# Attention and gated MLP on one core: the first two batches in turns of two f tiles, a written-out opening, and two DMA queues with fixed contents

## The chip, the cores and the metric

The kernel runs on one core of one Trainium2 chip. The metric is the device time of one execution in microseconds (us). Three runs of the kernel before took 806.85, 806.34 and 803.88 us, median 806.34.

The engines are named as in the profile: PE (TensorE matmuls; PEld its weight loads), DVE (VectorE), ACT (ScalarE), POOL (GpSimd, which in this kernel mainly issues DMAs) and SP (SyncE, which only issues DMAs).

## What is computed

Eight batches, eight heads, 576 tokens, head size 64; a learned memory of 32 slots per head; then a gated MLP of width 1536 on the 512 features of every token.

```python
a = softmax(phi)                       # over the 32 slots
k_m = einsum('bhsm,bhsd->bhmd', a, k)  # 32 keys and values per head
v_m = einsum('bhsm,bhsd->bhmd', a, v)
attn = softmax(q @ k_m.T / 8)
x = (attn @ v_m)                       # to [4608 tokens, 512]
out = (sigmoid(x @ w_gate) * (x @ w_val)) @ w_out
```

The weights of the MLP arrive as 64-bit words and are turned into 32-bit floats on the chip.

## The kernel before

**Tiles.** The 1536 columns of the MLP are 12 *f tiles* of 128. A *step* is one f tile of one batch. `make_u` (line 395 ff.) multiplies v_m into the gate and value weights of one or two f tiles, which gives `u` (in a high and a low part, `u_hi`, `u_lo`). `gate_half` (line 419) multiplies the attention weights `at` (again `at_hi`, `at_lo`) by `u`: half c=0 takes 256 tokens, half c=1 takes 320. ACT forms the sigmoid, DVE the product `sg` (line 445), ACT and DVE split it in `g_hi` and `g_lo`. `out_half` (line 455) multiplies that by the output weights `wo` and adds it up in four PSUM tiles acc0 to acc3 of 128 tokens, two to a half. It follows its gate half by three halves (`LAG`).

**Turns.** A batch is worked on for a stretch of f tiles, a *turn*. Batches 0 to 3 take turns of four f tiles (steps 0 to 47: batches 0, 1, 2, 3 with f 0 to 3, then all four with f 4 to 7, then with f 8 to 11), batches 4 to 7 one turn of twelve (steps 48 to 95). At the end of a turn the four sums leave PSUM: DVE or ACT write them to a `row` tile (lines 471 to 476; two buffers), which is stored to DRAM as `part`. At the end of the next turn of the batch `row_of` (line 489) loads that part again, DVE adds it (line 471), and the row is stored as `part` or `out`. The rows of acc0 and acc1 are loaded ahead; those of acc2 and acc3 need the buffers that the stores of the first two free. The next turn needs acc0 to acc3 again about two halves later. `at` has two buffers, so a batch that comes back has its `at` loaded again (`again`).

**Attention** of a batch is: `a_max` and `a_exp` (softmax over phi; DVE and ACT), `memory` (PE transposes, k_m and v_m, more transposes), `scores` (PE, DVE transposes into `e`), `s_max`, `s_exp`, `normalize` and `turn` (DVE and ACT), which gives `at`. From batch 1 on these pieces are fed between the halves of the steps of another batch (`sides`, `go_on`).

**Weights.** A conversion (`to_f32`, line 162; ACT one operation, DVE four) is due at the step that the table `CONVERT` gives: jobs (f, 0) and (f, 1) make the gate and value weights of f tile f, job (f, 2) its `wo` (a cast on ACT and a subtraction on DVE more). The words of the next job are loaded as soon as one of three `words` buffers is free (one buffer for the last f tiles).

**Order.** The first part, up to line 626, is written out as `step(...)` calls, each of which is chained behind the one before on PE, DVE, ACT and POOL. After that PE's matmuls and ACT's activations with a table are chained in program order, and a scheduler places the other instructions. All loads but those of `part` are chained on SP's queue in program order (`load`, line 112): phi, k and v, q, the words, and `at` coming back. The loads of `part` (line 493) are on SP's queue too, placed freely. Stores (`store`, line 119) are on POOL's queue, placed freely.

Of the kernel before, what the change touches and what calls it, by code (L numbers as in the profile page):

```python
# [17 lines left out]
P = 128  # L18
# [19 lines left out]
ALONE = 4  # L38
# [14 lines left out]
def attn_moe_kernel(  # L53
# [56 lines left out]
    last_load = [None]  # L110

    def load(dst, src):

        with ExitStack() as behind:
            if last_load[0] is not None:
                behind.enter_context(tc.issue_after(last_load[0].ins))
            last_load[0] = nc.sync.dma_start(dst, src)  # L117

    def store(dst, src):

        nc.gpsimd.dma_start(dst, src)  # L121
# [26 lines left out]
    def load_jobs(n=None):  # L148

        while jobs and (n is None or n > 0):  # L150
            f, k = jobs[0]
            room = WORDS[len(wos) - 1]
            if (k == 2 and f // NE >= len(wos)) or len(waiting) == room:
                break
            src = wo[f] if k == 2 else wgv[f][:, 2 * k : 2 * k + 2, :].rearrange("p k n -> p (k n)")
            words = pools["conv"].tile([P, 512, 2], I32, name="words", bufs=room)
            load(words.rearrange("p n t -> p (n t)"), src.bitcast(I32))
            words_of[f, k] = words
            waiting.append(jobs.pop(0))
            n = n and n - 1  # L160
# [41 lines left out]
    def load_phi(b):  # L202
        ph = att([P, NG, S], "ph")
        load(ph, phiT[b])
        loaded[b, "phi"] = ph

    def load_kv(b):
        kt = att([P, 512], "kvt")
        load(kt, kvt[b])
        km = []  # L210
        for g in range(NG):
            t = att([P, SF, 512], f"kvm{g}")
            load(t, kvm[b, g])
            km.append(t)
        loaded[b, "kv"] = (km, kt)

    def load_q(b, cuts=(0, 1)):
        if 0 in cuts:
            loaded[b, "q"] = att([P, NKT * S], "q")
        for c in cuts:  # L220
            for u, n in PIECES[c]:
                o = u * NKT * 2 * P
                load(loaded[b, "q"][:, o : o + NKT * n], qT[b][:, o : o + NKT * n])
# [134 lines left out]
    def turn(b, c=None):  # L358
# [26 lines left out]
    def again(b):  # L385
        new_at(b)
        for d, a in zip(kept[b], at[b]):
            load(a.rearrange("p r n -> p (r n)").bitcast(F32), d)
# [66 lines left out]
    def out_half(b, f, c, at_start, at_end):  # L455
# [3 lines left out]
        for j in range(2):  # L459
# [8 lines left out]
            if at_end:  # L468
# [8 lines left out]
                if f == NFT - 1:  # L477
                    store(out[b * S + t * P : b * S + (t + 1) * P, :], st)
# [10 lines left out]
    def row_of(b, t):  # L489

        st = mb.tile([P, DM], F32, name="row", bufs=2)
        if (b, t) in part:
            nc.sync.dma_start(st, part[b, t])
        return st
# [6 lines left out]
    def out_left(pair, f0, nf):  # L501
# [66 lines left out]
    turns = [(b, f0, f0 + TURN) for f0 in range(0, NFT, TURN) for b in range(QUAD)]  # L568
# [17 lines left out]
    load_jobs(1)  # L586
    load_kv(0)
    load_jobs(1)
    load_q(0)
    load_phi(1)  # L590
    load_jobs(1)
    load_kv(1)
    load_jobs()
# [87 lines left out]
    for b in range(QUAD, B - 1):  # L681
# [5 lines left out]
        begin[turns[k - 1][:2]]: b for k, (b, f0, _) in enumerate(turns) if b < QUAD and f0  # L687
# [15 lines left out]
    pend = []  # L703
    for i, (b, f, at_start, at_end) in enumerate(steps):
        if i in sides:
            run(beside)
            beside, pieces = chain(*(g for _, g in sides[i])), sum(n for n, _ in sides[i])
            length = next(n for n in range(i + 1, len(steps) + 1) if n == len(steps) or steps[n][2]) - i
            slots = 2 * length - 1
# [3 lines left out]
        if i:  # L713
            gate_half(b, f, 0)
# [11 lines left out]
        if i:  # L726
            gate_half(b, f, 1)
# [64 lines left out]
```

## Time and profile before

| | |
|---|---|
| median of three runs | 806.34 us |
| the profiled execution's own time | 808.47 us |
| its span, first to last instruction | 806.7 us |
| mean granted TensorE clock | 0.965 |
| PE busy | 745.8 us (92%) |
| DVE busy | 435.2 us (54%) |
| ACT busy | 338.9 us (42%) |
| POOL busy | 44.4 us (6%) |
| bytes moved | 93.17 MB |

A row of a timeline gives the start in us, the duration, the engine, the line, the operation, output<-inputs with their shapes, and in brackets how long the engine had been idle and who released it. A row of the windows gives a stretch, then busy time (and count) of PE, PEld, DVE, ACT and POOL, then the granted clock, the share of the DMA engines and GB/s. A DMA's row is its issue; when it landed is told in the sixth part of the page.

### The profile page before, as it was taken

Reading aid. Unit: us, or ns where it says so; the run is one execution under the profiler, and the core shown is the slowest. Engines: PE = TensorE matmul, PEld = TensorE weight load, DVE = VectorE, ACT = ScalarE, POOL = GpSimd, SP = SyncE. Lnnn points to the kernel's source line nnn. Section 1 sums busy time; section 2 is a strip of 40 time slices with the busy share of each in tenths; the row PEclk is TensorE's granted clock in tenths of the full one; section 3 lists DMA queues with packets and bytes.
Section 4 is the critical chain, followed back from the end, with each engine's and each line's share of the span. In section 5 each row is a group of like instructions: output and inputs, shape, how many; then the busy total and the mean of one; then the engine's idle time right before and its main releaser. Section 6 shows DMA issues by size and latency. Waiting matters only on the chain.

```text
span 806.7 us, 13723 instructions
## 1 busy us (share of the span) xinstructions
PE 745.8 (92%) x5588; PEld 615.0 (76%) x5588; DVE 435.2 (54%) x840; ACT 338.9 (42%) x791; POOL 44.4 (6%) x86
## 2 busy tenths in 40 slices
PE   7447789998999999999999999999999999999995
PEld 5335568786788877888888888878888888888884
DVE  4788485958646655454754653356234643343422
ACT  3456354644734334333444443336333443333321
POOL 0000010110100100110010100000000000010001
PEclk9669889999999999999999999999999999999998
DMA  9754627363663544343245233002000100010001
GB/s 351 275 185 172 256 87 302 121 240 127 250 242 118 200 171 147 116 143 107 79 137 187 79 102 119 1 27 86 2 1 1 53 14 1 1 53 1 1 1 66
DMA packets 26879, 93.17 MB, mean 115 GB/s; under 512 B 3520, under 2 KB 4544, under 8 KB 24768
## 3 DMA queue, kind: packets, MB, share of 16 engines
q1 hardware_dynamic: 20160, 69.74, 24.5%
q0 software_dynamic: 6656, 22.55, 7.5%
q8 instruction: 44, 0.72, 0.4%
q14 instruction: 19, 0.16, 0.1%
HBM read 69.73 MB, written 22.54 MB: 114 GB/s over the span
## 4 chain that ended last, share of the span: by engine, by line
PE 56%; issue 20%; DMA 9%; DVE 8%; ACT 5%; POOL 1%; SPq 1%; POOLq 0%; DVEq 0%; ACTq 0%
PE pu_t L135 34%; PE acc L135 21%; DMA words<-in_wo_dram 6%; DMA words<-in_wgv_dram 3%; ACT L108 2%; DVE wg L172 1%; DMA kvm<-in_kvm_dram 1%; POOL out_dram L121 1%; DVE wg L175 1%; ACT ph L108 1%; SPq L117 1%; ACT wo_raw L167 0%; DVE sg L445 0%; ACT wg L167 0%; DVE wg L168 0%
## 5 line engine op out<-in xcount | busy, mean ns | idle before, releaser
L135 PE MATMUL pu_t<-at_hi,u_hi 128*128 128x256 f32 (+1 forms) x760 | 230.4, 303 | 6.9 <-DVE sg L445 4.6
L135 PE MATMUL pu_t<-at_hi,u_lo 128*128 128x256 f32 (+1 forms) x760 | 226.2, 298 | 2.5 <-DVE u_lo L125 2.5
L135 PE MATMUL pu_t<-at_lo,u_hi 128*128 128x256 f32 (+1 forms) x760 | 226.2, 298 | 0.0
L445 DVE TENSOR_TENSOR sg<-pu_t,sg 128x256 f32<-128x256 f32 (+1 forms) x190 | 86.6, 456 | 203.6 <-ACT sg L108 117.4
L108 ACT ACTIVATE sg<-pu_t 128x256 f32<-128x256 f32 (+1 forms) x190 | 77.6, 410 | 216.8 <-PE pu_t L135 216.2
L135 PE MATMUL acc<-wo_hi,g_hi 128*128 128x512 f32 x384 | 157.6, 410 | 6.3 <-DVE row L476 3.8
L135 PEld LDWEIGHTS pu_t<-at_hi,u_hi 128*128 128x128 f32 x760 | 144.3, 190 | 21.0 <-DVE sg L445 6.1
L135 PE MATMUL acc<-wo_hi,g_lo 128*128 128x512 f32 x384 | 153.7, 400 | 0.0
L135 PE MATMUL acc<-wo_lo,g_hi 128*128 128x512 f32 x384 | 152.7, 398 | 0.0
L135 PEld LDWEIGHTS pu_t<-at_lo,u_hi 128*128 128x128 f32 x760 | 144.6, 190 | 7.2
L135 PEld LDWEIGHTS pu_t<-at_hi,u_lo 128*128 128x128 f32 x760 | 144.9, 191 | 2.9 <-DVE u_lo L125 2.9
L446 ACT CAST g_hi<-sg 128x256 fp32r<-128x256 f32 x192 | 78.0, 406 | 133.9 <-DVE sg L445 133.6
L135 PEld LDWEIGHTS acc<-wo_hi,g_hi 128*128 128x128 f32 x384 | 73.0, 190 | 55.2 <-issue 39.0
L125 DVE TENSOR_TENSOR g_lo<-sg,g_hi 128x256 fp32r<-128x256 f32 x192 | 81.0, 422 | 61.3 <-ACT g_hi L446 61.2
L135 PEld LDWEIGHTS acc<-wo_hi,g_lo 128*128 128x128 f32 x384 | 72.9, 190 | 17.0
L135 PEld LDWEIGHTS acc<-wo_lo,g_hi 128*128 128x128 f32 x384 | 73.1, 190 | 9.3
L125 DVE TENSOR_TENSOR u_lo<-pu_t,u_hi 128x512 fp32r<-128x512 f32 (+1 forms) x100 | 63.3, 664 | 2.6 <-ACT u_hi L404 0.7
L135 PE MATMUL pu_t<-wg,vT 64*32 64x512 f32 (+1 forms) x800 | 55.3, 589 | 2.8 <-DVE wg L175 2.8
L404 ACT CAST u_hi<-pu_t 128x512 fp32r<-128x512 f32 (+1 forms) x100 | 51.7, 569 | 4.2 <-PE pu_t L135 4.0
L121 POOL DMA_DIRECT2D out_dram<-row x32 | 17.4, 543 | 409.8 <-DVE row L476 289.9
L121 POOL DMA_DIRECT2D part<-row x32 | 17.5, 548 | 210.5 <-DVE row L471 110.9
L471 DVE TENSOR_TENSOR row<-acc,row 128x512 f32<-128x512 f32 x32 | 22.0, 687 | 8.3 <-DMA row<-part 7.3
(92 smaller groups left out, 606.3 us busy)
## 6 DMA issues: line engine op xcount, KB each, us to landing
kvm<-in_kvm_dram SPq DMA_DIRECT2D x16, 1024.0 KB, 8.7
words<-in_wgv_dram SPq DMA_DIRECT2D x24, 512.0 KB, 5.6
q<-in_qT_dram SPq DMA_DIRECT2D x16, 512.0 KB, 5.6
part<-row POOLq DMA_DIRECT2D x32, 256.0 KB, 2.5
row<-part SPq DMA_DIRECT2D x32, 256.0 KB, 2.8
out_dram<-row POOLq DMA_DIRECT2D x32, 256.0 KB, 2.3
words<-in_wo_dram SPq DMA_DIRECT2D x12, 512.0 KB, 5.9
ph<-in_phiT_dram SPq DMA_DIRECT2D x8, 576.0 KB, 5.4
```

The lines of the kernel that those rows point to most:

```text
L108: last_act[0] = nc.scalar.activation(*args, **kw)
L117: last_load[0] = nc.sync.dma_start(dst, src)
L121: nc.gpsimd.dma_start(dst, src)
L125: nc.vector.tensor_tensor(lo, x, hi.bitcast(F32), op=ALU.subtract)
L135: last_pe[0] = do(*args, **kw)
L172: nc.vector.scalar_tensor_tensor(bits, high, -0x40000000, bits, op0=ALU.bitwise_and, op1=ALU.bitwise_or)
L175: nc.vector.scalar_tensor_tensor(bits, low, 29, bits, op0=ALU.logical_shift_right, op1=ALU.bitwise_or)
L404: nc.scalar.copy(hi[:, r, :nf], pb[r])
L445: nc.vector.tensor_tensor(prod[:, :n], ps[1][:, :n], sg[:, :n], op=ALU.mult)
L446: nc.scalar.copy(ghi, prod[:, : 2 * P])
L471: nc.vector.tensor_tensor(st, o, st, op=ALU.add)
```

## The change

**Turns.** Batches 0 and 1 take f 0 to 3 in two turns of two f tiles each, in the order batch 0 f 0, 1; batch 1 f 0, 1; batch 0 f 2, 3; batch 1 f 2, 3. Batches 2 and 3 keep their turns of four, and from f 4 on nothing changes in the order of steps. Steps 0 to 15 hold the same (batch, f) pairs as before in another order. Two more turns end with sums that are stored and added up later.

**Opening.** The written-out part now holds steps 0 and 1 whole, all of batch 1's attention (`a_max` to `turn`), the conversion (0, 2) and `make_u` of batch 1's first pair. `a_max` and `a_exp` of batch 1 stand ahead of batch 0's `normalize`. The loop starts at step 2, the table `CONVERT` and the table `sides` are rewritten to fit: batch 2's memory beside steps 2 and 3, its scores beside steps 4 to 7, batch 3's memory and scores beside steps 8 to 11. `ALONE` (f tiles of batch 0 whose `u` is made one at a time) goes from 4 to 2.

**Queues.** `load` and `store` become one `move` with a queue of its own order each. On SP's queue, chained: phi, k and v, q, `at` out and back, and the first three words. On POOL's queue, chained: all other words, and the rows of sums, out and back.

```diff
-ALONE = 4
+ALONE = 2
...
+    queues = {"batch": nc.sync, "stream": nc.gpsimd}
+    last_move = {}
+
+    def move(dst, src, queue="batch"):
...
+            if queue in last_move:
+                behind.enter_context(tc.issue_after(last_move[queue].ins))
+            last_move[queue] = queues[queue].dma_start(dst, src)
...
-    def load_jobs(n=None):
+    def load_jobs(n=None, queue="stream"):
...
-                store(d, a.rearrange("p r n -> p (r n)").bitcast(F32))
+                move(d, a.rearrange("p r n -> p (r n)").bitcast(F32))
...
-                    store(part[b, t], st)
+                    move(part[b, t], st, "stream")
...
-            nc.sync.dma_start(st, part[b, t])
+            move(st, part[b, t], "stream")
...
-    turns = [(b, f0, f0 + TURN) for f0 in range(0, NFT, TURN) for b in range(QUAD)]
+    half = TURN // 2
+    turns = [(b, f0, f0 + half) for f0 in range(0, TURN, half) for b in range(2)]
+    turns += [(b, 0, TURN) for b in range(2, QUAD)]
+    turns += [(b, f0, f0 + TURN) for f0 in range(TURN, NFT, TURN) for b in range(QUAD)]
...
     step(s_exp, 0, 1)
+    step(a_max, 1)
+    step(a_exp, 1)
     step(normalize, 0, 0)
...
+    piece(m1, 3)
     step(convert, 1, 0)
+    step(gate_half, 0, 0, 1)
     step(convert, 1, 1)
+    piece(m1, 3)
+    load_phi(2)
+    load_kv(2)
+    step(make_u, *u_at.pop(0))
+    step(scores, 1, 0)
+    step(scores, 1, 1)
+    step(gate_half, 0, 1, 0)
+    step(s_max, 1)
+    step(gate_half, 0, 1, 1)
...
+    step(convert, 0, 2)
...
+    step(normalize, 1)
+    step(turn, 1)
+    load_q(2)
...
+    step(make_u, *u_at.pop(1))
...
-        0: [(6, m1), (1, phis(2)), (4, score(1, 2)), (2, attend(1)), (6, remember(2, True))],
-        begin[1, 0]: [(4, score(2, 3)), (2, attend(2)), (6, remember(3, True))],
-        begin[2, 0]: [(4, score(3)), (2, attend(3))],
+        2: [(8, remember(2))],
+        4: [(4, score(2, 3)), (2, attend(2))],
+        begin[2, 0]: [(6, remember(3, True)), (4, score(3)), (2, attend(3))],
```

**What moves, in three places.** The first is DVE's list in the opening, between `u_lo` of the first f tile and `at_lo` of batch 0's first tokens. Before:

```order
L125 TENSOR_TENSOR u_lo<-pu_t,u_hi 128x256 x2
L348 TENSOR_REDUCE zs<-e 128x2x8
L349 TENSOR_SCALAR zs<-zs 128x2x8
L350 RECIPROCAL zs<-zs 128x2x8
L351 TENSOR_TENSOR e<-e,zs 128x2x256
L374 STREAM_TRANSPOSE u_hi<-e 128x256 x2
L125 TENSOR_TENSOR at_lo<-u_hi,at_hi 128x2x256
```

The same place in the changed kernel, whose lines have other numbers (`nmx` is the maximum over batch 1's phi, `z` the sum of its exponentials, `rz` one over it):

```order
L123 TENSOR_TENSOR u_lo<-pu_t,u_hi 128x256 x2
L228 TENSOR_REDUCE nmx<-ph 128x2
L241 TENSOR_SCALAR z<-z 128x2
L242 RECIPROCAL rz<-z 128x2
L346 TENSOR_REDUCE zs<-e 128x2x8
L347 TENSOR_SCALAR zs<-zs 128x2x8
L348 RECIPROCAL zs<-zs 128x2x8
L349 TENSOR_TENSOR e<-e,zs 128x2x256
L372 STREAM_TRANSPOSE u_hi<-e 128x256 x2
L123 TENSOR_TENSOR at_lo<-u_hi,at_hi 128x2x256
```

Three instructions of batch 1 now stand ahead of batch 0's softmax; the second of them needs ACT's exponentials of the whole of batch 1's phi.

The second place is the end of batch 0's turn f 8 to 11, on the queue that loads parts. Before, this is SP's list (`part_2` and `part_3` belong to acc2 and acc3; the stores are on POOL):

```order
L493 DMA row<-part_1_7_2473 128x512
L117 DMA at_hi<-at_0_1099 128x1152
L117 DMA at_lo<-at_1_1100 128x1152
L493 DMA row<-part_2_7_2525 128x512
L493 DMA row<-part_3_7_2533 128x512
```

Now it is POOL's list, with the stores of the sums in it:

```order
L119 DMA row<-part_0_7_2511 128x512
L119 DMA row<-part_1_7_2517 128x512
L119 DMA out_dram<-row 128x512 x2
L119 DMA row<-part_2_7_2569 128x512
L119 DMA out_dram<-row 128x512
L119 DMA row<-part_3_7_2577 128x512
L119 DMA out_dram<-row 128x512
```

The load for acc3 stands behind the store of acc2's row, where before it stood right behind the load for acc2.

The third place is DVE's list at the same turn end (the four `row<-acc` are acc0 to acc3 in this order). Before:

```order
L471 TENSOR_TENSOR row<-acc_3464,row 128x512
L125 TENSOR_TENSOR g_lo<-sg,g_hi 128x256
L471 TENSOR_TENSOR row<-acc_3468,row 128x512
L445 TENSOR_TENSOR sg<-pu_t,sg 128x256
L125 TENSOR_TENSOR g_lo<-sg,g_hi 128x256
L125 TENSOR_TENSOR u_lo<-pu_t,u_hi 128x512 x2
L471 TENSOR_TENSOR row<-acc_3492,row 128x512
L471 TENSOR_TENSOR row<-acc_3496,row 128x512
L445 TENSOR_TENSOR sg<-pu_t,sg 128x320
```

Now:

```order
L469 TENSOR_TENSOR row<-acc_3508,row 128x512
L123 TENSOR_TENSOR g_lo<-sg,g_hi 128x256
L469 TENSOR_TENSOR row<-acc_3512,row 128x512
L443 TENSOR_TENSOR sg<-pu_t,sg 128x256
L123 TENSOR_TENSOR g_lo<-sg,g_hi 128x256
L123 TENSOR_TENSOR u_lo<-pu_t,u_hi 128x512 x2
L469 TENSOR_TENSOR row<-acc_3536,row 128x512
L443 TENSOR_TENSOR sg<-pu_t,sg 128x320
L123 TENSOR_TENSOR g_lo<-sg,g_hi 128x256
L443 TENSOR_TENSOR sg<-pu_t,sg 128x256
L469 TENSOR_TENSOR row<-acc_3540,row 128x512
```

The addition for acc3 stands three instructions further back, behind the products of the next two halves.

More of the change, by code (lines that the diff above doesn't have):

```diff
@@ L156, in load_jobs @@
             words = pools["conv"].tile([P, 512, 2], I32, name="words", bufs=room)
-            load(words.rearrange("p n t -> p (n t)"), src.bitcast(I32))
+            move(words.rearrange("p n t -> p (n t)"), src.bitcast(I32), queue)
             words_of[f, k] = words
@@ L203, in load_phi @@
         ph = att([P, NG, S], "ph")
-        load(ph, phiT[b])
+        move(ph, phiT[b])
         loaded[b, "phi"] = ph
@@ L208, in load_kv @@
         kt = att([P, 512], "kvt")
-        load(kt, kvt[b])
+        move(kt, kvt[b])
         km = []
@@ L212, in load_kv @@
             t = att([P, SF, 512], f"kvm{g}")
-            load(t, kvm[b, g])
+            move(t, kvm[b, g])
             km.append(t)
@@ L222, in load_q @@
                 o = u * NKT * 2 * P
-                load(loaded[b, "q"][:, o : o + NKT * n], qT[b][:, o : o + NKT * n])
+                move(loaded[b, "q"][:, o : o + NKT * n], qT[b][:, o : o + NKT * n])
     def a_max(b):
@@ L387, in again @@
         for d, a in zip(kept[b], at[b]):
-            load(a.rearrange("p r n -> p (r n)").bitcast(F32), d)
+            move(a.rearrange("p r n -> p (r n)").bitcast(F32), d)
     U = {}
@@ L477, in out_half @@
                 if f == NFT - 1:
-                    store(out[b * S + t * P : b * S + (t + 1) * P, :], st)
+                    move(out[b * S + t * P : b * S + (t + 1) * P, :], st, "stream")
                 else:
                     part[b, t] = dram.tile([P, DM], F32, name=f"part{b}_{t}_{f}")
-                    store(part[b, t], st)
+                    move(part[b, t], st, "stream")
                 del acc[b, t]
@@ L522, in out_left @@
                 b = 2 * pair + j
-                store(out[b * S + SF * P : (b + 1) * S, :], st[j * TAIL : (j + 1) * TAIL, :])
+                move(out[b * S + SF * P : (b + 1) * S, :], st[j * TAIL : (j + 1) * TAIL, :], "stream")
         yield
@@ L585, in attn_moe_kernel @@
     load_phi(0)
[L586 removed]
+    load_jobs(1, "batch")
     load_kv(0)
[L588 removed]
+    load_jobs(1, "batch")
     load_q(0)
     load_phi(1)
[L591 removed]
+    load_jobs(1, "batch")
     load_kv(1)
[L593 removed]
     m0, m1 = memory(0), memory(1)
@@ L686, in attn_moe_kernel @@
     returns = {
-        begin[turns[k - 1][:2]]: b for k, (b, f0, _) in enumerate(turns) if b < QUAD and f0
+        begin[turns[k - 1][:2]]: b for k, (b, f0, _) in enumerate(turns) if b < QUAD and f0 >= TURN
     }
@@ L701, in go_on @@
         slots -= 1
-    pend = []
+    pend = [(b, f, c, at_start, at_end) for b, f, at_start, at_end in steps[:2] for c in range(2)]
+    for half in pend[:2]:
+        out_half(*half)
+    del pend[:2]
     for i, (b, f, at_start, at_end) in enumerate(steps):
+        if i < 2:
+            del U[b, f]
+            continue
         if i in sides:
@@ L707, in attn_moe_kernel @@
             beside, pieces = chain(*(g for _, g in sides[i])), sum(n for n, _ in sides[i])
-            length = next(n for n in range(i + 1, len(steps) + 1) if n == len(steps) or steps[n][2]) - i
-            slots = 2 * length - 1
+            until = next(n for n in range(i + 1, len(steps) + 1) if n in sides or n == len(steps) or n > 8 and steps[n][2])
+            slots = 2 * (until - i) - 1
         if i in returns:
@@ L718, in attn_moe_kernel @@
         if i in u_at:
-            if steps[i + 1][0] != b:
+            if steps[i + 1][2] and (steps[i + 1][1] == 0 or i > 2 * QUAD):
                 run(beside)
```

26 lines of the change are left out of this document (7 added, 19 removed), and 8 rows, old and new, of the table CONVERT.

## The prediction

> **What bounds the kernel now.** I read the page, then the busy time by stretch, then who PE waited for, then the timelines where the change touches them. First the page's busy line, and the windows cut where steps 0, 3, 8 and 16 begin (26.29, 90.86, 139.3 and about 201 us):
>
> ```profile
> PE 745.8 (92%) x5588; PEld 615.0 (76%) x5588; DVE 435.2 (54%) x840; ACT 338.9 (42%) x791; POOL 44.4 (6%) x86
> ```
>
> ```profile
> core 0: us, PE busy (x) PEld busy (x) DVE busy (x) ACT busy (x) POOL busy (x), PEclk, DMA share, GB/s
> 0.00:26.29 26.29, 15.59 (x210) 10.88 (x210) 14.22 (x30) 9.58 (x21) 0.69 (x6) 0.95 0.94 365
> 26.29:90.86 64.57, 38.96 (x377) 29.68 (x377) 49.15 (x96) 33.66 (x65) 2.38 (x4) 0.74 0.49 174
> 90.86:139.30 48.44, 44.05 (x379) 36.02 (x376) 27.99 (x49) 24.46 (x54) 3.24 (x6) 0.92 0.60 231
> 139.30:201.07 61.77, 57.12 (x402) 46.52 (x402) 48.64 (x96) 31.76 (x69) 5.41 (x10) 0.97 0.47 170
> ...
> 320.00:806.70 486.70, 477.22 (x3434) 398.50 (x3432) 223.09 (x423) 187.28 (x454) 23.84 (x44) 1.00 0.17 59
> ```
>
> From 320 us on PE is the bound (477.22 of 486.70). Only the first 200 us have slack: three steps take the whole stretch from 26.29 to 90.86, with PE busy 60% at 0.74 of its clock, while DVE is busy 76%. There the bound is DVE's list and what it waits for. The waits of PE from 26.3 to 201 us say which:
>
> ```profile
> PE acc L135 <- ACT at_hi L375: 9.8, 2, 6.1
> PE pu_t L135 <- ACT ph L108: 9.7, 2, 6.7
> PE pu_t L135 <- ACT e L259: 4.5, 1, 4.5
> PE acc L135 <- DVE row L476: 3.8, 1, 3.8
> PE pu_t L135 <- DVE u_lo L125: 3.3, 3, 1.6
> PE pu_t L135 <- DVE sg L445: 3.0, 3, 1.9
> ```
>
> Nearly all end with an operation of the attention or of a conversion. What a step costs when PE never waits is read from POOL's stores at two turn ends, four steps apart: 352.85 - 326.47 = 26.38, or 6.6 us a step.
>
> ```profile
> 326.47 0.54 POOL L121 DMA_DIRECT2D part<-row  x1 [16.88 <-DVE row L471]
> 352.85 0.54 POOL L121 DMA_DIRECT2D out_dram<-row  x1 [16.93 <-DVE row L471]
> ```
>
> **The change part by part.** *The first gate.* Batch 1's maximum, the wait for its exponentials and two small operations now stand on DVE ahead of batch 0's softmax. The rows of before, where they stood later, and of the place they go to:
>
> ```profile
> 22.88 0.68 DVE L348 TENSOR_REDUCE zs<-e 128x16 f32<-128x512 f32 x1
> 45.78 1.35 DVE L230 TENSOR_REDUCE nmx<-ph 128x2 f32<-128x1152 f32 x1
> 49.75 0.78 ACT L108 ACTIVATE ph<-ph,nmx 128x576 f32<-128x576 f32 x1
> 51.19 0.19 ACT L108 ACTIVATION_READ_ACCUMULATOR ph<-ph,nmx 128x1 f32 x1
> 51.41 0.17 DVE L243 TENSOR_SCALAR z<-z 128x2 f32<-128x2 f32 x1 [1.24 <-ACT ph L108]
> 26.29 0.58 PE L135 MATMUL acc<-at_hi,u_hi 128*128 128x256 f32 x1 [6.13 <-ACT at_hi L375]
> ```
>
> That is 1.35, then 1.6 on ACT (49.75 to 51.38), then 0.35: 3.3 us, all on the path to the matmul at 26.29, which nothing covers. The words that GpSimd now loads at about 10 us share the DMA engines with k, v and q at 0.94 of their capacity: 0 to 1.3 us (512 KB at the 365 GB/s of that stretch), and I take 0.9. The first gate comes 4.2 later.
>
> *To step 3.* Before step 3 DVE has the same work in both kernels: eight weight conversions, three of `wo`, two batches' attention, the products of three steps. So I keep the time of before, 64.57, and correct it. The 1.7 of batch 1's maximum and sums already done come off. The words of f 2 go through one buffer, each load issued when the conversion before it has ended: two waits of about 1 us on a landing of some 4, bounds 0 and 2 x 4. Batch 3's maximum waits for a phi that is loaded when PE has turned batch 2's: 2, bounds 0 and 5. Sum: 4.2 - 1.7 + 2 + 2 = 6.5 later at step 3, with the same attention and conversions left. The new cover, batch 1's two steps, does not help, since its own attention has to pass through DVE first, and the scheduler has set four conversions among its instructions.
>
> *Steps 3 to 15.* Before, PE lost here 3.8 on rows, 3.3 on `u_lo` and 1.9 on `sg`, and after some of these waits ran at half clock. The longest wait has a cause that goes:
>
> ```profile
> 172.68 10.76 SPq L117 DMA_DIRECT2D words<-in_wgv_dram  x2
> 187.49 0.60 PE L135 MATMUL acc<-wo_hi,g_hi 128*128 128x512 f32 x1 [3.80 <-DVE row L476]
> ```
>
> The words of `wo` stood behind q and `at` on SP, DVE waited for them with the row's copy queued behind, and PE then ran ten matmuls at half speed: 3.8 + 2.0 = 5.8 saved. Conversions of f 4 and 5 move into steps 4 to 6, where DVE has room (27.99 of 48.44): I take 3 off the smaller waits, bounds 0 and 8. Against that stand two more turn ends that load parts (batches 0 and 1, f 2 and 3). By the chain below, with DVE late there, batch 0's makes PE wait about 4.5 in step 8 and batch 1's 1: 5.5, bounds 0 and 9. The eight copies and additions more on DVE (0.69 each) hide in that room. Step 16 then begins 6.5 - 5.8 - 3 + 5.5 = 3.2 later.
>
> *The turn ends from f 4 on.* Nothing changes in their steps, only in their queue. Four timelines of the end of batch 0's turn f 8 to 11, DVE, POOL, SP and PE:
>
> ```profile
> 351.86 0.69 DVE L471 TENSOR_TENSOR row<-acc,row 128x512 f32<-128x512 f32 x1
> ...
> 357.96 0.69 DVE L471 TENSOR_TENSOR row<-acc,row 128x512 f32<-128x512 f32 x1 [0.84 <-DMA row<-part]
> 359.47 0.69 DVE L471 TENSOR_TENSOR row<-acc,row 128x512 f32<-128x512 f32 x1 [0.81 <-DMA row<-part]
> ```
>
> ```profile
> 358.95 0.54 POOL L121 DMA_DIRECT2D out_dram<-row  x1 [4.63 <-DVE row L471]
> ```
>
> ```profile
> 355.19 7.93 SPq L493 DMA_DIRECT2D row<-part  x4
> ```
>
> ```profile
> 360.99 0.40 PE L135 MATMUL acc<-wo_hi,g_hi 128*128 128x512 f32 x1
> ...
> 361.69 0.39 PE L135 MATMUL acc<-wo_hi,g_hi 128*128 128x512 f32 x1
> ```
>
> The load for acc2 is issued at 355.19 and used at 357.96, 2.77 later. The load for acc3 ran beside it. Now it waits in POOL's list for the store of acc2's row: that is issued at 358.95 and takes 0.54, the load then 2.77, DVE's addition 0.69, so acc3 is free at 362.95 and not at 360.16. PE wants it at 361.69. A slack of 1.5 becomes a wait of 1.3. What is queued behind: on PE the next half's gate, on DVE the `g_lo` and `sg` of the next halves, whose lag of three halves covers it.
>
> A load of rows by POOL's queue is not in the trace. Its bounds come from the page's landings:
>
> ```profile
> part<-row POOLq DMA_DIRECT2D x32, 256.0 KB, 2.5
> row<-part SPq DMA_DIRECT2D x32, 256.0 KB, 2.8
> out_dram<-row POOLq DMA_DIRECT2D x32, 256.0 KB, 2.3
> ```
>
> Two loads stand in that chain, so 2.3 gives a wait of 0.4; SP's slowest, 4.6 (a busy queue), would give 5. I take 2.77, the same data in the same direction. The Trainium skill ("DMA: Bandwidth & Descriptors", section "Anatomy of one DMA — SWDGE (gpsimd) path") gives a DMA from this queue 2.0 us plus its bytes at 436 GB/s, which by estimate is 2.6 for 256 KB; by it the wait would be about 1.0 and this term a quarter smaller. The stores' rows of 2.3 and 2.5 agree with it roughly.
>
> There are eight such ends. At those of batches 1 and 3, f 8 to 11, the 24 matmuls of the leftover tokens stand in between (0.233 each from 360.99 to 361.69, 5.6 in all), so there it costs nothing. Batch 2's there has pieces of batch 5's memory: 0.6. Three are like the one shown: 3.9. At the other two, batches 1 and 2 with f 4 to 7, PE already waited for these rows:
>
> ```profile
> 277.85 0.50 PE L135 MATMUL acc<-wo_hi,g_hi 128*128 128x512 f32 x1 [0.97 <-DVE row L471]
> 308.81 0.50 PE L135 MATMUL acc<-wo_hi,g_hi 128*128 128x512 f32 x1 [1.52 <-DVE row L471]
> ```
>
> There the whole delay of 2.8 would come on top, unless DVE's conversions were the cause and hide part: 1.3 to 2.8, I take 2.0 each, 4.0. Words loads that stand in the list ahead of acc2's load are in that. Sum 8.5, bounds 1 and 22.
>
> *Clock.* After a wait PE may run at half clock for some 3 us. Two rows show that it need not:
>
> ```profile
> 214.76 0.41 PE L135 MATMUL pu_t<-at_hi,u_hi 128*128 128x320 f32 x1 [1.39 <-DVE u_lo L125]
> 216.29 0.63 PE L135 MATMUL acc<-wo_hi,g_hi 128*128 128x512 f32 x1
> 302.60 0.41 PE L135 MATMUL pu_t<-at_hi,u_hi 128*128 128x320 f32 x1 [1.61 <-DVE sg L445]
> ```
>
> After the first the matmuls take 0.63 in place of 0.39, after the second they don't slow down. I take one such spell of 1.7 among the new waits, bounds 0 and 8. The Trainium skill ("TensorE: Matmul & The Clock Gate", section "HAM oscillation — how this bites in real kernels") asks only that PE never idle for more than about 3.4 us; by that none of the waits of 1.3 would cost clock. The row at 214.76 speaks against it.
>
> **The sum.** 3.2 + 8.5 + 1.7 = 13.4 on the profiled span of 806.7 gives 820.1; the execution's own time lies 1.77 above its span, 821.9; the median of the runs lies 2.13 below the profiled execution. So I forecast 819.7, say 819. A measurement of this kernel can tell about 0.5%, 4 us, from no change.
>
> **The rivals.** *The opening pays (faster).* Work of two batches keeps DVE fed: its share up to step 3 rises from 76% to 90%, 49.15 / 0.9 = 54.6, 10 us earlier. For it: the long waits above are for single operations of one batch. Against it: the new waits in DVE's list, and that DVE's work is the same. With the 5.8 and 3 saved, 5.5 lost, and 1.3 at only three turn ends (3.9): -10 - 5.8 - 3 + 5.5 + 3.9 = -9.4, a time of about 797. It decides if batch 2's first gate, at 139.3 now, begins before 128.
>
> *The queue is hidden (no change).* Loads from POOL's queue land in 2.3, as its stores do, the late ends cost 1 to 2, the opening comes out even: 806 to 809. For it: 0.4 a wait is within the slack that side pieces give. Against it: the 2.8 of the same loads now.
>
> *Every wait costs clock (much slower).* Each of eight waits is followed by half clock as at 214.76, 1.7 each, 12 more than I took, and the step-3 delay stays: 819 + 12 + 3 = 834. For it: 0.74 in the opening's row. Against it: the row at 302.60.
>
> **How the numbers follow.** Forecast 0.47 (813 to 826), opening pays 0.18, hidden 0.17, clock 0.18. Between 799 and 832 about half of the first and the last rival is left out. Faster by over 0.5% is the opening that pays: 0.18. Within it: the hidden queue, 0.17. Slower: 0.65. The slower cases alone reach from 812 to 834.
>
> **What would show it.** Right: the first gate at about 30.5; step 3 (the first gate half of batch 1's second f tile) near 97; batch 2's first gate near 135 with batch 3's memory still to come; step 16 near 204; at the ends of turns from f 4 on PE waits of 1 to 3 us for the row of acc3, with a load of its part issued after a store on POOL. Wrong: rows that land before PE wants acc3, or step 16 before 195. If step 16 is late but the turn ends are clean, the opening was mis-sized and the queue priced for nothing.

## The result, and the profile after

The changed kernel takes 859.9 us (median of four runs, 858.8 to 862.9) against 806.6: 1.0675 times as long, 95% interval 1.0638 to 1.0712. The direction was forecast, the size was not: 53 us slower where 13 were expected, far above the range. The profiled execution has a span of 857.1 us (before: 806.7).

First the busy line of the page, and its landings:

```profile
PE 762.7 (89%) x5584; PEld 625.9 (73%) x5584; DVE 442.9 (52%) x846; ACT 338.7 (40%) x789; POOL 83.7 (10%) x159
...
words<-in_wgv_dram POOLq DMA_DIRECT2D x21, 512.0 KB, 5.9
part<-row POOLq DMA_DIRECT2D x40, 256.0 KB, 2.6
row<-part POOLq DMA_DIRECT2D x40, 256.0 KB, 3.2
```

PE has 17 us more of busy time for the same matmuls: part of the loss is clock, not waiting. The windows, cut where steps 0, 3, 8, 16 and 32 begin:

```profile
core 0: us, PE busy (x) PEld busy (x) DVE busy (x) ACT busy (x) POOL busy (x), PEclk, DMA share, GB/s
0.00:29.48 29.48, 16.06 (x210) 10.51 (x210) 15.80 (x33) 11.26 (x26) 1.92 (x8) 0.87 0.94 368
29.48:95.16 65.68, 38.45 (x372) 30.41 (x372) 43.63 (x79) 29.64 (x56) 4.97 (x10) 0.72 0.43 152
95.16:136.69 41.53, 37.96 (x284) 30.26 (x281) 32.66 (x60) 23.16 (x49) 7.70 (x14) 0.96 0.56 204
136.69:216.99 80.30, 66.35 (x495) 54.42 (x493) 51.45 (x99) 33.63 (x74) 14.04 (x26) 0.87 0.66 230
354.50:857.10 502.60, 484.85 (x3434) 403.75 (x3432) 223.14 (x423) 187.58 (x454) 33.54 (x62) 0.98 0.17 57
```

The first matmul of a step's first gate half, in us, with the distance from before in brackets, shows where it was lost. The last column is the run with the change's turns and opening but the queues of before, told of below.

| step | before | after | turns alone |
|---|---|---|---|
| 0 | 26.29 | 29.48 (+3.2) | 29.61 (+3.3) |
| 3 | 90.86 | 95.16 (+4.3) | 89.42 (-1.4) |
| 8 | 139.14 | 136.69 (-2.4) | 129.55 (-9.6) |
| 11 | 161.69 | 183.10 (+21.4) | 166.39 (+4.7) |
| 16 | 200.91 | 216.99 (+16.1) | 200.30 (-0.6) |
| 36 | 346.37 | 384.87 (+38.5) | 343.98 (-2.4) |
| 52 | 476.63 | 529.59 (+53.0) | 474.25 (-2.4) |

After step 52 nothing more is lost. There are two stretches of loss: 24 us between steps 8 and 11, and 37 from step 16 to step 52, where turns end. Whom PE waited for, from 95 to 217 us:

```profile
PE acc L133 <- DVE row L469: 10.5, 3, 4.2
PE pu_t L133 <- DVE u_lo L123: 5.7, 2, 3.3
PE pu_t L133 <- DVE sg L443: 1.3, 1, 1.3
```

And from 217 us on (before, from 201 us on, it waited 2.5 us for rows):

```profile
PE acc L133 <- DVE row L469: 27.8, 10, 5.8
```

**One late turn end.** These are the timelines of the end shown in the prediction, batch 0 with f 8 to 11. POOL, then DVE, then PE:

```profile
391.34 0.54 POOL L119 DMA_DIRECT2D out_dram<-row  x1 [15.79 <-DVE row L469]
392.28 0.55 POOL L119 DMA_DIRECT2D out_dram<-row  x1 [0.39 <-DVE row L469]
394.41 0.54 POOL L119 DMA_DIRECT2D row<-part  x1 [1.59 <-DMA out_dram<-row]
398.38 0.54 POOL L119 DMA_DIRECT2D out_dram<-row  x1 [3.42 <-DVE row L469]
398.91 0.54 POOL L119 DMA_DIRECT2D row<-part  x1
```

```profile
397.39 0.69 DVE L469 TENSOR_TENSOR row<-acc,row 128x512 f32<-128x512 f32 x1 [1.77 <-DMA row<-part]
...
402.13 0.69 DVE L469 TENSOR_TENSOR row<-acc,row 128x512 f32<-128x512 f32 x1 [1.54 <-DMA row<-part]
```

```profile
402.88 0.50 PE L133 MATMUL acc<-wo_hi,g_hi 128*128 128x512 f32 x1 [2.52 <-DVE row L469]
...
404.53 0.47 PE L133 MATMUL pu_t<-at_hi,u_lo 128*128 128x320 f32 x1
...
407.93 0.39 PE L133 MATMUL acc<-wo_lo,g_hi 128*128 128x512 f32 x1
```

The order is the one foreseen: acc3's load (398.91) stands behind the store of acc2's row (398.38). The wait is 2.52 and not 1.3. DVE itself idles 1.54 us for that load ahead of the addition at 402.13, so the load holds it and not the addition's place in DVE's list. Then matmuls of 320 columns take 0.47 (a full-speed one takes 0.31). The clock granted in these 3 us:

```profile
404.50:407.50 3.00, 3.00 (x11) 2.81 (x11) 0.49 (x1) 0.70 (x2) 0.54 (x1) 0.50 0.57 168
```

So a turn end costs 4.3 us here (step 38 to step 40: +38.5 to +42.8), 2.5 of it the wait.

### The profile page after: what moved, and what is told of

The parts are those of the page before. It is cut to its first block, busy times and chain, and to the rows that moved or that the text cites. A ratio compares the mean times of both kernels' runs of the same rounds, so it can differ in the third digit from the quotient of the medians.

```text
span 857.1 us, 13688 instructions
## 1 busy us (share of the span) xinstructions
PE 762.7 (89%) x5584; PEld 625.9 (73%) x5584; DVE 442.9 (52%) x846; ACT 338.7 (40%) x789; POOL 83.7 (10%) x159
## 4 chain that ended last, share of the span: by engine, by line
PE 38%; issue 29%; DMA 15%; DVE 8%; ACT 7%; POOL 2%; SPq 0%; POOLq 0%; DVEq 0%; ACTq 0%
PE pu_t L133 24%; PE acc L133 15%; DMA words<-in_wgv_dram 6%; DMA row<-part 4%; DMA words<-in_wo_dram 2%; DVE row L469 2%; ACT L108 1%; DMA part<-row 1%; ACT wg L165 1%; POOL part L119 1%; ACT ph L108 1%; POOL out_dram L119 1%; DVE sg L443 1%; ACT e L108 1%; DMA kvm<-in_kvm_dram 1%
## 5 line engine op out<-in xcount | busy, mean ns | idle before, releaser
L133 PE MATMUL pu_t<-at_hi,u_hi 128*128 128x320 f32 (+1 forms) x756 | 232.5, 308 | 14.3 <-ACT u_hi L402 6.1
L133 PE MATMUL pu_t<-at_lo,u_hi 128*128 128x320 f32 (+1 forms) x756 | 228.5, 302 | 1.2 <-DVE at_lo L123 1.2
L133 PE MATMUL pu_t<-at_hi,u_lo 128*128 128x320 f32 (+1 forms) x756 | 228.2, 302 | 0.1
L133 PE MATMUL acc<-wo_hi,g_hi 128*128 128x512 f32 x384 | 161.8, 421 | 51.6 <-DVE row L469 38.2
L443 DVE TENSOR_TENSOR sg<-pu_t,sg 128x320 f32<-128x320 f32 (+1 forms) x189 | 86.2, 456 | 206.4 <-PE pu_t L133 103.3
L108 ACT ACTIVATE sg<-pu_t 128x320 f32<-128x320 f32 (+1 forms) x189 | 77.4, 410 | 233.6 <-PE pu_t L133 233.4
L133 PE MATMUL acc<-wo_hi,g_lo 128*128 128x512 f32 x384 | 155.9, 406 | 0.0
L133 PE MATMUL acc<-wo_lo,g_hi 128*128 128x512 f32 x384 | 155.3, 405 | 0.0
L133 PEld LDWEIGHTS pu_t<-at_hi,u_lo 128*128 128x128 f32 x756 | 146.8, 194 | 0.6 <-DVE u_lo L123 0.6
L119 POOL DMA_DIRECT2D part<-row x40 | 21.8, 545 | 188.9 <-DVE row L469 122.0
L469 DVE TENSOR_TENSOR row<-acc,row 128x512 f32<-128x512 f32 x40 | 27.4, 686 | 24.4 <-DMA row<-part 23.3
```

Of the source, the lines that this page charges most:

```text
L108: last_act[0] = nc.scalar.activation(*args, **kw)
L119: last_move[queue] = queues[queue].dma_start(dst, src)
L133: last_pe[0] = do(*args, **kw)
L443: nc.vector.tensor_tensor(prod[:, :n], ps[1][:, :n], sg[:, :n], op=ALU.mult)
```

## The experiments

The theory after the result: **the queue.** The loads of parts, the stores that they wait for and the words stand in one list, and whatever stands behind a store waits for a sum; the clock adds to each wait. The rivals: the turns and the opening lose the time, or DVE's order does. Ratios are against the kernel before on the same chip, with intervals.

| run | ratio | interval |
|---|---|---|
| changed kernel | 1.0675 | 1.0638 to 1.0712 |
| e1 loads of part on SP | 1.0399 | 1.0375 to 1.0422 |
| e2 before, rows in GpSimd's list | 1.0428 | 1.0410 to 1.0447 |
| e3 pair of loads | 1.0342 | 1.0323 to 1.0361 |
| e4 before, words on GpSimd | 1.0129 | 1.0111 to 1.0146 |
| e5 added sums left out | 1.0579 | 1.0557 to 1.0601 |
| e6 turns alone | 1.0022 | 1.0007 to 1.0036 |
| e7 queues alone | 1.0379 | 1.0348 to 1.0410 |
| e8 before, late words on GpSimd | 1.0041 | 1.0025 to 1.0057 |
| e9 turns alone, four row buffers | 1.0012 | 0.9998 to 1.0026 |
| e10 pair of loads, words on SP | 1.0169 | 1.0149 to 1.0189 |
| e11 waits filled | 1.0552 | 1.0532 to 1.0572 |
| e12 as e9, first gate early | 1.0025 | 1.0010 to 1.0040 |
| e13 as e6, batch 4's data late | 1.0060 | 1.0037 to 1.0082 |
| e14 as e9, batch 3's memory early | 1.0075 | 1.0051 to 1.0098 |
| e15 both of these | 1.0039 | 1.0017 to 1.0060 |

### e1: the loads of parts back on SP's queue

```diff
-            move(st, part[b, t], "stream")
+            nc.sync.dma_start(st, part[b, t])
```

> The changed kernel with one line back: the loads of part are issued on SP's queue, placed freely, as before the change. Queue theory (the loads of part that stand behind stores in GpSimd's list, and the words that stand behind both, make nearly all of the 53 us): the waits of PE for the rows of acc2 and acc3 from 260 us on go (22.5 us of waits and the half clock behind them, 34 us between step 16 and step 64), the 23 us lost between step 8 and step 11 shrink to the 5 of the two added turn ends: about 860 - 34 - 13 = 813. Rival, the new turns and opening are to blame for what is lost before step 16 and the queue only for what comes after: 860 - 34 = 826. Rival, DVE's order at the turn ends makes the rows late whatever the queue: about 860.

838.8 us: 21 came back, of 34 to 47 that were expected. From step 34 on nothing is lost any more, so for the turn ends of f 8 to 11 the queue is the cause. Before step 16 nothing came back (step 16 at 223.64, 6.7 later than in the changed kernel). Words still stand behind stores on GpSimd:

```profile
154.76 0.54 POOL L119 DMA_DIRECT2D part<-row  x1 [0.39 <-DVE row L469]
155.29 0.54 POOL L119 DMA_DIRECT2D words<-in_wgv_dram  x1
```

The load at 155.29 is the sixteenth of the words, for the second half of f 5's gate and value weights. The table sets their conversion at step 12, but the scheduler has put it into ACT's list ahead of a `u_hi` in step 9, which began at 155.86; PE then waits 3.33 us for the `u_lo` that follows this `u_hi`.

### e2: the kernel before, with rows out and back in one list of GpSimd's

```diff
-        nc.gpsimd.dma_start(dst, src)
+        with ExitStack() as behind:
+            if last_row[0] is not None:
+                behind.enter_context(tc.issue_after(last_row[0].ins))
+            last_row[0] = nc.gpsimd.dma_start(dst, src)
...
-            nc.sync.dma_start(st, part[b, t])
+            store(st, part[b, t])
```

> The kernel before with one thing of the change: rows of sums, out and back, in one list of GpSimd's in program order. Turns, opening and words as before. Queue theory: PE waits about 2.3 us for the row of acc3 at the turn ends from f 4 on, and some 1.7 us of half clock follow most of these: about 806 + 34 = 840, and nothing changes before step 16. Rival, the loss needs the words in the same list or the new turns: 806 to 812.

840.8 us, as the theory had it. At step 16 this kernel stands within 0.1 us of before, and at step 52 it is 28.4 late. The list's order, added to a kernel that is otherwise unchanged, makes the late loss by itself. Its waits at the same places:

```profile
348.17 0.50 PE L140 MATMUL acc<-wo_hi,g_hi 128*128 128x512 f32 x1 [2.20 <-DVE row L476]
...
416.09 0.50 PE L140 MATMUL acc<-wo_hi,g_hi 128*128 128x512 f32 x1 [2.00 <-DVE row L476]
...
490.27 0.50 PE L140 MATMUL acc<-wo_hi,g_hi 128*128 128x512 f32 x1 [2.00 <-DVE row L476]
```

### e3: the two loads next to each other

```diff
-                st = rows.pop((b, t), None) or row_of(b, t)
+                if t == 2:
+                    rows[b, 2], rows[b, 3] = row_of(b, 2), row_of(b, 3)
+                st = rows.pop((b, t))
```

> The changed kernel with its queues, but the loads for acc2 and acc3 stand next to each other in the list, ahead of the store of acc2's row. Queue theory: acc3's load is issued at once behind acc2's, some 4 us earlier, so acc3 is free before PE wants it at most turn ends: the 34 us after step 16 nearly go; before step 16 the words still stand behind stores, so a half of the 23 stays: 860 - 34 - 10 = 816, within 812 to 830. Rival, loads of GpSimd's queue are slow whatever stands ahead of them (it is the queue and not its order): 850 to 860.

834.4 us: 25.5 of the 53 come back with one load moved past one store. POOL at the same turn end:

```profile
384.77 1.23 POOL L119 DMA_DIRECT2D row<-part  x2 [1.35 <-DMA out_dram<-row]
388.72 0.55 POOL L119 DMA_DIRECT2D out_dram<-row  x1 [2.72 <-DVE row L471]
```

From step 34 on no loss is left, though the loads of this queue land no sooner (3.3 us, page). There it is the order in the list, not the queue's speed. Between steps 28 and 32, at batch 2's turn end, 11.0 us are still lost: there a words load stands ahead of the pair (below). The loss before step 16 stays, 18 us where the changed kernel has 16; I had expected half.

### e4: the kernel before, with the words on GpSimd's queue

```diff
-            load(words.rearrange("p n t -> p (n t)"), src.bitcast(I32))
+            put(words.rearrange("p n t -> p (n t)"), src.bitcast(I32))
```

where `put` is a chain of its own on GpSimd, but for the first three words.

> The kernel before with the words (all but the first three) on GpSimd's queue, in a list of their own order; stores stay placed freely and the loads of part stay on SP. If the words themselves are well placed there: the wait of 3.8 us at 187.49 and the half clock behind it go, 806 - 5.8 = 800 to 806. Rival, words on GpSimd's queue crowd the opening or stand behind stores: PE's waits before step 16 grow, 808 to 820.

817.3 us, the rival's side. Stores are not in the words' chain here, and the jam of before at 187.49 is gone, but steps 4 to 8 take longer: step 4 is 2.4 late, step 8 is 12.5 late, and 6.4 of that comes back later. PE's waits there:

```profile
121.73 0.64 PE L135 MATMUL pu_t<-at_hi,u_hi 128*128 128x320 f32 x1 [4.26 <-ACT sg L108]
134.61 1.94 PE L135 MATMUL pu_t<-kvm,e 128*32 128x128 f32 x32 [5.17 <-ACT e L268]
```

The last words of this kernel are loaded at 226.4 us and in the kernel before at 303.2. Conversions of later f tiles now stand among batch 2's attention and batch 3's memory on ACT and DVE: from 100 to 160 us ACT starts eleven of them, before four. That the scheduler does this because it reckons with words that land earlier is likely and not shown.

### e5: the added turn ends' sums left out

```diff
-            if at_end:
+            if at_end and f == 1:
+                del acc[b, t]
+            elif at_end:
...
-        if (b, f + 1) in ends and c:
+        if (b, f + 1) in ends and c and f:
```

> The changed kernel, with the sums of the two added turn ends (batches 0 and 1, f 1) left out: they are not copied, stored, loaded or added, so f 0 and 1 of these two batches are missing from the output. It measures what the added turn ends cost before step 16. If their rows make the loss between step 8 and step 11: the waits of 2.78, 4.23 and 3.46 us for rows go with the half clock behind them, about 14 us: 860 - 14 = 846. Rival, words and conversions come late there and would hold PE anyway: 855 to 860.

852.9 us, half of what the first theory expected. The three row waits (10.5 us) are gone, and of these 24 us between steps 8 and 11 only 7 remain; but step 12 is still 12.6 late and step 16 11.7. Other places move with the edit too: step 3 comes 8 us later than in the changed kernel, which is won back by step 8. The next waits were ready:

```profile
157.16 0.64 PE L133 MATMUL pu_t<-at_hi,u_hi 128*128 128x320 f32 x1 [2.61 <-DVE u_lo L123]
181.54 0.58 PE L133 MATMUL pu_t<-at_hi,u_hi 128*128 128x256 f32 x1 [5.08 <-ACT at_hi L373]
```

### e6: turns and opening alone

The changed kernel with `load_jobs`, `store` and `row_of` of before: words on SP's chain, stores and loads of parts placed freely.

> Turns, opening and tables of the change with the queues of before: words chained on SP, loads of part on SP and stores on GpSimd, both placed freely. Theory (the turns have a loss of their own before step 16, the rest is the queues): late turn ends clean; before step 16 the row waits of step 8 stay (4.75 and 1.53 with the rows on SP), the wait for words (3.3) goes: 838.8 of the run with the rows on SP, less 3 to 12: 826 to 836. Rival, all of the loss is the queues' and the turns come out even: 803 to 812.

807.5 us, the rival: turns, opening and tables together cost 0.2% (interval 0.07 to 0.36%). With the queues of before, 1.5 of the 53 us are left, and nothing is lost at step 16 (-0.6). Step 3 begins 1.4 earlier than before and not 4.3 later, with the same opening written out. In the changed kernel batch 1's `at_lo` comes later on DVE, since from 38 us on eight conversions begin ahead of it and not six. DVE in the changed kernel, then in this one:

```profile
73.16 0.43 DVE L166 TENSOR_SCALAR wg<-wg 128x512 f32<-128x512 f32 x1 [0.38 <-ACT wg L165]
...
79.97 1.35 DVE L123 TENSOR_TENSOR at_lo<-q,at_hi 128x1152 fp32r<-128x1152 f32 x1
```

```profile
67.19 0.41 DVE L170 TENSOR_SCALAR wo_raw<-wo_raw 128x512 f32<-128x512 f32 x1
...
73.27 1.36 DVE L127 TENSOR_TENSOR at_lo<-q,at_hi 128x1152 fp32r<-128x1152 f32 x1 [0.65 <-ACT at_hi L377]
```

This kernel is 9.6 ahead at step 8 and 4.7 behind at step 11, with 7.24 us of that in one wait for a row of an added turn end. So of the 24 us that the changed kernel loses between these steps the turns alone lose 14 as well. What the queues add before step 16 is 16.7: 7.2 up to step 8 and 9.5 from there to step 11.

### e7: the queues alone

The kernel before with `move`, the words and the rows in one GpSimd list and `at` on SP's.

> Queues of the change (words and rows in one list of GpSimd's, at on SP's) with the turns, the opening and the tables of before. If the two parts that were run alone add up: rows in the list gave 28.4 us at step 64, words on GpSimd 6.1: 806 + 34.5 = 841. Rival, they are worse together, since words then stand behind stores that wait for sums: 848 to 860.

835.8 us, below both figures. The two parts together cost less than e2 alone, and e4's cost doesn't come on top (30 us against 34 and 10). At step 16 nothing is lost (-0.5), all of it at the turn ends behind it. So the loss before step 16 in the changed kernel needs the new queues and the new turns together. In all, the queues cost 30 us with the turns of before and 52 with the new ones (859.9 against e6): the new turns cost 1.5 with the old queues, and 24 with the new.

### e8: only the words of f 6 to 11 on GpSimd's queue, in the kernel before

```diff
+            (load if f < 6 else load_words)(words.rearrange("p n t -> p (n t)"), src.bitcast(I32))
```

> The kernel before with only the words of f 6 to 11 on GpSimd's queue; all else as before. They then don't stand behind q and at on SP's queue at 170 us. If the queue makes the wait of 3.80 us for the row at 187.49: it goes with the half clock behind it, 806 - 5 = 801. Rival, the transfers themselves are too many at that place (about 3.2 MB from 168 us on), whichever queue issues them, or the conversions pulled forward hold DVE: 806 to 810.

809.5 us, the rival. The wait of 3.80 at 187.49 shrinks to 2.22, and two new ones, 3.01 and 2.01 us for batch 3's `at_hi` and `at_lo`, stand at 172 to 175. As in e4, earlier words go with earlier conversions: ACT starts five between 150 and 175 us, where before it starts none between 146.8 and 178.9. That these make the two new waits is likely and not shown.

### e9 and e12: four row buffers, and the first gate early

```diff
-            for t in range(2):
-                rows[b, t] = row_of(b, t)
+            for t in range(4 if f < TURN else 2):
+                rows[b, t] = row_of(b, t, f < TURN and t >= 2)
```

In e12 `a_max` and `a_exp` of batch 1 also stand behind batch 0's last `turn`.

> The kernel with the change's turns and the queues of before, and with two more row buffers at the turn ends of f 1 and f 3 (in the space that the words' last buffers leave early), so that the parts of all four sums are loaded ahead and none waits for a store. Theory: the added turn ends cost what their rows' chain store, load, addition costs: PE's waits of 1.67 and 7.24 us for rows at 132.8 and 160.2 go, with some half clock: 807.5 - 9 - 2 = about 797. Rival, the DMA engines are full there (0.99 from 141 to 155 us), so the rows come late in any buffer, or batch 3's attention is next: 803 to 808.

> As the run with two more row buffers, and batch 1's maximum and exponentials stand behind batch 0's turn instead of ahead of its softmax. If the 3.3 us that the first gate lost count: first gate at 26.3, and 2 to 3 us less than that run. Rival, batch 1's memory starts as much later and step 2 doesn't move: no difference.

e9: 807.6 us. The waits of 1.67 and 7.24 for rows are gone, and step 16 begins at 199.90 where it began at 200.30: the lead goes to waits for `sg`, `u_lo` and batch 3's `at_hi`. The rival was right in its second half. e12: 809.5. The first gate is back at 26.28 and the second step begins later for it, at 49.16 instead of 46.51; the 3.3 us of the first gate were worth nothing.

### e10: the pair of loads, and the words back on SP

```diff
-    def load_jobs(n=None, queue="stream"):
+    def load_jobs(n=None, queue="batch"):
```

> The changed kernel with the loads for acc2 and acc3 next to each other (834.4 alone) and the words back on SP's queue; rows, out and back, stay in one list of GpSimd's. Theory, the loss has two parts, the store ahead of acc3's load and the words on GpSimd's queue: both are gone, 806 to 812. Rival, rows in one list still hold PE before step 16, where the waits of 2.71 and 3.16 us stood: 816 to 826.

820.9 us: 13 less than e3, so the words in the list were a second part, and 13 more than e6, so the rows in a fixed list are a third, as the rival had it (the stores of `at`, on SP's queue here and on GpSimd's in e6, are in that difference too). Here is the largest early wait, for a row of an added turn end:

```profile
140.53 0.80 PE L133 MATMUL acc<-wo_hi,g_hi 128*128 128x512 f32 x1 [6.16 <-DVE row L471]
```

In this order of undoing, the 53 us are 25.5 for the one load behind a store, 13.4 for the words, 13.4 for the rest of the rows' list with the stores of `at`, and 1.0 for turns and opening. In another order the parts come out otherwise (e1 and e6: 21 for the loads of parts, 31 for the words among the stores and `at` on SP), since a late word hides behind a late row.

### e11: the waits filled

```diff
+            if at_start and t == 3 and (b, f) in filled:
+                idle = bank()
+                for _ in range(FILL):
+                    matmul(idle[:, :256], spare[:, :P], spare, start=True, stop=True)
```

`filled` are the eight turn starts after an end with f 4 or more, FILL is 20.

> The changed kernel with 20 matmuls on an unread tile ahead of acc3's first matmul at the eight turn starts that wait for its row: some 2 us of PE work that lies in the wait. Theory, the wait itself slows TensorE's clock for some 3 us afterwards: the waits are filled, the clock stays up, about 1.7 us less at five or six of the eight: 860 - 9 = 851. Rival, the slow spell has another cause, or the filling comes on top: 858 to 868.

850.9 us: 9 less, with 160 matmuls more. The same turn end:

```profile
394.17 0.39 PE L134 MATMUL acc<-wo_lo,g_hi 128*128 128x512 f32 x1
394.40 0.40 PE L134 MATMUL acc<-wo_hi,g_lo 128*128 128x512 f32 x1
394.63 2.36 PE L134 MATMUL pu_t<-ident 128*128 128x256 bf16 x20
397.33 0.51 PE L134 MATMUL acc<-wo_hi,g_hi 128*128 128x512 f32 x1 [0.34 <-DVE row L474]
...
399.47 0.31 PE L134 MATMUL pu_t<-at_hi,u_hi 128*128 128x320 f32 x1
```

acc3's row comes no sooner, but PE idles 0.34 us instead of 2.52, and the matmuls after it keep 0.31. Step 38 to step 40 loses 2.9 and not 4.3. Of the eight ends only batch 2's with f 4 to 7, where PE still idles 5.65 us for acc2's row, has slow matmuls left. So the second part of a turn end's cost is the clock that follows an idle PE.

### e13, e14 and e15: where the lead at step 8 goes

e13 loads batch 4's phi, k and v at step 13; e14 puts batch 3's memory beside steps 4 to 7; e15 does both. e14 and e15 have e9's row buffers.

```diff
-        4: [(4, score(2, 3)), (2, attend(2))],
-        begin[2, 0]: [(6, remember(3, True)), (4, score(3)), (2, attend(3))],
+        4: [(4, score(2, 3)), (2, attend(2)), (6, remember(3, True))],
+        begin[2, 0]: [(4, score(3)), (2, attend(3))],
```

> The run with the turns alone (807.5), with batch 4's phi, k and v loaded at step 13 instead of at the end of batch 3's memory. If these transfers make the rows late: the wait of 7.24 us at 160 shrinks by half, step 12 begins 4 us earlier, 803. Rival, batch 3's attention is due then anyway, or the words of steps 13 to 16 now stand behind these transfers: 806 to 812.

> The run with four row buffers (807.6), with batch 3's memory beside steps 4 to 7 instead of steps 8 to 11. If batch 3's attention takes the lead: the waits for sg, u_lo and at_hi at 146.9, 149.0, 169.3 and 170.8 (6.2 us) shrink, step 12 begins 4 to 6 us earlier, 802. Rival, steps 4 to 7 get as much longer: 806 to 810.

> Both: batch 3's memory beside steps 4 to 7, batch 4's phi, k and v loaded at step 13, four row buffers. If both take a part of the lead: 798 to 801. Rival, what is gained is given back at the words of steps 13 to 16: 805 to 810.

811.1, 812.9 and 810.0 us: none keeps the lead. Step 16 begins at 203.7, 202.4 and 204.4, against 200.30 in e6 and 200.91 before. In e13 the 7.24 is gone and waits of 2.12 and 2.06 come elsewhere; in e14 steps 4 to 7 get 15 us longer than in e9 (4.25 of it a wait for ACT's `sg` at 117.84) and steps 8 to 11 only 7 shorter. What sets step 16 at about 200 us in all these orders stays open; no run here beats the kernel before.

## Why the prediction was wrong, point by point

**The turn ends from f 4 on: right mechanism, wrong size, and two ends wrongly set at nothing.** The term was 8.5; from step 16 to step 52 the kernel lost 36.9. Per end it came to 2.3, 5.7, 10.8 and 4.0 (f 4 to 7) and 4.3, 3.9, 4.0 and 2.3 (f 8 to 11). Three steps of the working failed:

- *"that is issued at 358.95 and takes 0.54, the load then 2.77"*: the chain starts later and each load takes longer. acc2's load is issued 3.07 after the first store (391.34 to 394.41; before, 352.85 to 355.19, 2.34), is used 2.98 later and acc3's 3.22 later. Together 1.3 became 2.1 to 2.5 at the three ends like this one. I had taken SP's landings (2.8) as the nearest row; GpSimd's loads land in 3.2. The estimate of 2.6 by the Trainium skill ("DMA: Bandwidth & Descriptors", section "Anatomy of one DMA — SWDGE (gpsimd) path") lay further off still.
- *"the 24 matmuls of the leftover tokens stand in between ... so there it costs nothing"*: they stand ahead of acc2's last matmul, so they delay the sum, the store and the load behind it, and cover nothing. Batch 1's end, DVE then POOL then PE:

```profile
433.64 0.68 DVE L469 TENSOR_TENSOR row<-acc,row 128x512 f32<-128x512 f32 x1
...
439.58 0.68 DVE L469 TENSOR_TENSOR row<-acc,row 128x512 f32<-128x512 f32 x1
```

```profile
425.39 0.54 POOL L119 DMA_DIRECT2D row<-part  x1 [1.12 <-DMA out_dram<-row]
434.62 0.54 POOL L119 DMA_DIRECT2D out_dram<-row  x1 [8.68 <-DVE row L469]
435.15 0.54 POOL L119 DMA_DIRECT2D row<-part  x1
```

```profile
440.32 0.50 PE L133 MATMUL acc<-wo_hi,g_hi 128*128 128x512 f32 x1 [2.00 <-DVE row L469]
```

  acc2's part was called for at 425.39; acc3's load followed 9.8 us later, behind acc2's sum and store.
- *"Words loads that stand in the list ahead of acc2's load are in that"* (2.0 each): at batch 2's end with f 4 to 7 a words load holds up the list for 2.45 us, with acc2's load behind it (it is issued 0.6 us after DVE's last operation on the words before, so it presumably waits for the one buffer); at batch 1's a words load of twice the size goes out just ahead of acc2's. Both rows come late at both. Undoing it bears this out: at batch 2's end (steps 28 to 32) 11.0 us are lost with the pair of loads (e3) and 3.0 with the words on SP's queue besides (e10). Batch 2's end, POOL, then PE:

```profile
330.42 0.54 POOL L119 DMA_DIRECT2D words<-in_wo_dram  x1 [2.45 <-issue]
330.94 0.54 POOL L119 DMA_DIRECT2D row<-part  x1
```

```profile
336.21 0.79 PE L133 MATMUL acc<-wo_hi,g_hi 128*128 128x512 f32 x1 [5.79 <-DVE row L469]
...
340.94 0.80 PE L133 MATMUL acc<-wo_hi,g_hi 128*128 128x512 f32 x1 [3.09 <-DVE row L469]
```

**The clock.** The price of one spell, 1.7, was right: matmuls are slow for about 3.4 us (404.4 to 407.9) at 0.50. The count was wrong: one was taken, and six of the eight ends have one (at the two where PE waits for both rows the clock stays at 0.50 for longer, in part while PE idles); filling the waits gave 9 us back (e11). That every wait costs clock was a rival at 0.18; it had the mechanism, and too small a wait to go with it. The Trainium skill ("TensorE: Matmul & The Clock Gate", section "HAM oscillation — how this bites in real kernels") asks that PE not idle for more than about 3.4 us; by that waits of 2.0 to 2.5 us are free. The rows disagree: 2.00 to 2.52 us of idling was enough at four of six ends; 2.09 at 268.21 and 2.00 at 514.84 cost no clock, and what sets these two apart stays open.

**The words: a step that failed for want of a place in the list.** They were priced as landings, 2 us ahead of step 3, and as a part of the 2.0 at two turn ends; before step 16 nothing was put for their place behind stores. But they stand in one list with the rows: behind two stores that wait for sums, the words for the second half of f 5's gate and value weights are issued at 155.77, though DVE had finished with all words before them at 129.1, so that a buffer was free. Three of the four conversions of f 4 and 5 ran early, as forecast (ACT at 104, 112 and 120 us). The fourth, set by the table at step 12, stands on ACT ahead of a `u_hi` in step 9, which waits behind it:

```profile
163.40 0.66 ACT L165 ACTIVATE wg<-words 128x512 f32<-128x512 f32 x1 [2.31 <-DMA words<-in_wgv_dram]
163.96 1.06 ACT L402 CAST u_hi<-pu_t 128x512 fp32r<-128x512 f32 x2
```

Ahead of step 3 they cost by another way, conversions pulled in front of batch 1's attention (e6: step 3 at 89.42 instead of 95.16, with six conversions and not eight ahead of that attention's `at_lo`; e4 shows such a cost with the turns of before, from step 4 on).

**The added turn ends.** 5.5 was taken, bounds 0 and 9; the row waits alone are 10.5 (2.78, 4.23, 3.46). Without these sums the kernel gains 7 (e5), as other late things stand right behind. With the queues of before, turns and opening cost 1.5 in all (e6).

**What was right, and what of it was luck.** The first gate (+3.2 against +4.2): the 3.3 of the three instructions was right, and the 0.9 for words that share the DMA engines was nothing (e7, with these words on GpSimd and the old order, has its first gate at 26.30; 512 KB at 365 GB/s are also 1.4 and not 1.3). But it led to nothing: *"all on the path to the matmul at 26.29, which nothing covers"* is true of that matmul, and e12 shows that the steps behind don't come earlier with it. Step 3 (95 against 97) and step 8 (136.7 against 135) came near the forecast by luck: 4.2 of the 6.5 at step 3 was the first gate's, and e6, with the same late first gate, has step 3 1.4 earlier than before. The jam of `wo` words, 5.8: from step 14 to step 15 the changed kernel wins back 5.6 (+21.4 to +15.8). The new queue is not needed for that: e7 (queues alone) wins back 5.6 there, and so does e6 with the words still on SP's queue (5.3). The rival that the opening pays hung on batch 2's first gate before 128; alone, the turns reach 129.55, and the lead is not kept.

## What to carry to other kernels

When transfers get an order of their own on one queue, go through that list entry by entry and write down what each waits for before it can be issued: a load behind a store inherits the store's wait for its sum, and a weight load behind both inherits all of it. Price the chain store, load, addition from its first event, and see whether work that seems to lie inside it delays its start. Add to each wait of PE of 2 us the slow matmuls that may follow it: here 1.7 us in four of six cases, and gone when unread matmuls filled the wait.

## What the runs showed of the hardware

- After PE had idled 2.0 to 2.5 us, the granted clock was 0.50 for about 3.4 us at four of six turn ends of the changed kernel. 2.4 us of matmuls put in the gap kept it at 1.00 (e11).
- Loads of 256 KB issued on GpSimd's queue landed in 3.2 us (median of 40), those on SP's in 2.8 (before, 32). Stores on GpSimd's took 2.3 to 2.6.
- A queue choice alone changed the order on DVE and ACT: in the kernel before, with only the words moved to GpSimd (e4), the last of them are issued 77 us earlier, conversions stand ahead of attention that they stood behind, and the kernel is 1.3% slower.
